# Mask addresses, a reordered tail and one filler matmul less in a decode-attention kernel that streams K and V

## The chip, the cores and the metric

The kernel runs on one core of one Trainium2 chip. The metric is the device time of one execution in microseconds (us). Single runs of one kernel spread over about 1.5 us (before beside e5 to e8: 629.71 to 631.37; e3: 629.97 to 631.48), and this case is about effects of that size, so most of the argument rests on times inside the traces and not on the totals. PE is the matmul engine, DVE the vector engine, ACT the scalar engine; SP issues the loads, and 16 DMA engines carry them out. PE's granted clock is what the trace says that PE ran at: in these traces either full (1.00) or half (0.50); a window that holds a change shows a value between.

## The reference

Grouped-query attention for one new token: 32 query heads share 8 K/V heads, 65,536 keys, head size 128, bf16. The arithmetic is small; K and V are 268.4 MB.

```python
B, Hq, Hkv, Sq, Sk, D = 1, 32, 8, 1, 65536, 128
k = jnp.repeat(k, rep, axis=1); v = jnp.repeat(v, rep, axis=1)
scores = jnp.einsum("bhqd,bhkd->bhqk", q, k) * D ** -0.5
return jnp.einsum("bhqk,bhkd->bhqd", softmax(scores), v)
```

## The kernel before

Each head's keys are cut into two loads (b = 0, 1) of 8.39 MB, laid out as 128 partitions by 256 slots of 128 values. There are two K buffers and one V buffer. All loads are issued by the sync engine (SP) in the order K(g,0), V(g-1,0), K(g,1), V(g-1,1), each as soon as its buffer is free:

```python
def load_k(g, b):
    SP.wait((s_sc, 16 * g - 8 + 8 * b if g else 0))     # scores of the old K are done
...
def load_v(g, b):
    done = 2 * (2 * g + b)
...
        SP.wait((s_vc, done))                            # PE has consumed the old V
        load(v, g, b, 0, s_v[0])
...
for g in range(1, G):
    for b in range(2):
        load_k(g, b)
        load_v(g - 1, b)
```

PE runs a loop over tiles x = 2g+b. A tile is eight parts of scores (eight matmuls each, on K that DVE has transposed in place), then the V matmuls of tile x-2. The addresses of a part come from two counters. The loop body for V has "wide" matmuls (four slots at once, 16 output rows in each of four column groups), and between its first and second half two *filler* matmuls whose result nobody reads:

```python
with block("pe_part"):
    nc.regs_alu(r_n, r_n, 1, op=ALU.add)
    ...
    r_k = (x % 2) * (SL * D) + (n // 2) * (PS * D) + (n % 2) * (2 * D) + SL * D
    r_w = (n % 4) * (-8) + 28
    r_o = (x % 2) * 1024 + (n // 4) * 512
    take(s_kt, 1)                       # wait for the transpose, subtract 1
    ...                                 # eight matmuls at these addresses
with block("pe_values"):
    ...
        if ch == 1:
            i.then_inc(s_vc, 1)
            for _ in range(2):          # the fillers
                pe.matmul(out=pt[0:16, :], lhsT=et[:, 0, 0:16], rhs=et[:, 0, :], start=True, stop=True)
    i.then_inc(s_vb, 1)                 # DVE may fold the wide sums
```

In the last tile V arrives in pieces that end at slots 128, 192, 224, 232, 240, 248, 252, 256. Slots 0 to 231 go through the wide matmuls; their sums are then folded on DVE ("y-sum": a multiply by a 0/1 mask and a reduce over y) and added to the output by the fp32 *gather* matmul. Slots 232 to 255 go one by one through narrow matmuls (4 output rows) straight into the output:

```python
for t in range(SL - TAIL, SL):          # TAIL = 24
    if t == CUTS[5]:
        ...                             # pl: the row sum, fp32
    if t in CUTS:
        pe.wait_ge(s_v[CUTS.index(t)], 16)
    ...                                 # narrow matmul of slot t
pe.wait_ge(s_dv, collected[G - 1])
gather(D, start=False, stop=True).then_inc(s_pe, 1)
```

## Time and profile before

| | before |
|---|---|
| median of 6 runs (lowest to highest) | 630.23 us (629.99 to 630.80) |
| span of the profiled run | 628.0 us |
| load queue, share of 16 engines | 99.1% |
| PE / DVE busy | 56% / 54% |
| last V bytes land | about 624.2 us |
| last matmul ends | 625.33 us |

First some lines of the profile page: the span, PE's busy time (us, share, instructions), the busy share of the DMA engines in 40 slices (tenths), the queue that carries all loads, and the median time from the issue of a full K load to its landing.

```profile
span 628.0 us, 6627 instructions
...
PE 352.5 (56%) x2136; PEld 138.0 (22%) x2136; DVE 339.2 (54%) x131; ACT 36.1 (6%) x32; POOL 7.5 (1%) x40
...
DMA  8999999999999999999999999999999999999996
...
q1 hardware_dynamic: 6656, 268.45, 99.1%
...
io<-in_k_dram SPq DMA_DIRECT2D x13, 43.3
```

The busy digits of DMA are 9 from the second slice to the last but one: the loads bound this kernel, and only what lies before the first and after the last byte, or makes the queue pause, can change the time.

The second view is the timeline of the last 14 us (start, duration, engine, line, operation, output<-input, count, and in brackets the idle time before it and what ended it).

```profile
614.73 3.59 PE L370 MATMUL acc<-io,et 128*16 128x512 bf16 x32 [6.13 <-PEq L113]
...
618.10 1.06 PE L432 MATMUL pt<-et 128*16 128x512 bf16 x2
...
619.63 1.04 PE L370 MATMUL acc<-io,et 128*16 128x512 bf16 x16 [0.47 <-PEq L113]
...
622.03 1.06 PE L370 MATMUL acc<-io,et 128*16 128x512 bf16 x10 [1.36 <-DMA io<-in_v_dram]
...
623.14 0.69 DVE L274 TENSOR_TENSOR vy<-acc,sely 128x512 f32<-128x512 f32 x1 [11.94 <-PE acc L370]
...
623.38 0.61 PE L465 MATMUL pf<-io,et 128*4 128x128 bf16 x8 [0.29 <-DMA io<-in_v_dram]
...
623.86 1.03 DVE L278 TENSOR_REDUCE vs<-vy 128x128 f32<-128x512 f32 x1
...
624.04 1.06 PE L465 MATMUL pf<-io,et 128*4 128x128 bf16 x16
...
624.95 0.38 PE L364 MATMUL pf<-vs,sel 128*4 128x128 f32 x2
625.43 0.36 ACT L331 ACTIVATE o<-pf,rl 4x128 bf16<-4x128 f32 x1 [31.86 <-PE pf L364]
```

Read it by line: L370 are the wide matmuls (32 of slots 0-127 when the first half has landed at 614.73, 16 at 619.63, ten from 622.03), L432 the fillers, L274 and L278 the y-sum, L465 the narrow matmuls, L364 the gather.

The third view is the same timeline around 173 us, in the steady state: the last parts of scores, then the issue of V(1,1), then the moment at which DVE begins on the K load that was the last one in flight.

```profile
165.32 1.92 PE L405 MATMUL acc<-io,wz 128*128 x8 [0.66 <-issue]
...
167.85 1.91 PE L405 MATMUL acc<-io,wz 128*128 x8 [0.61 <-issue]
...
173.80 0.33 SPq L131 DMA_DIRECT2D io<-in_v_dram  x1
...
178.85 4.45 DVE L227 STREAM_TRANSPOSE io<-io 128x4096 uint32<-128x4096 uint32 x1 [21.34 <-DMA io<-in_k_dram]
```

A part takes 2.53 us (165.32 to 167.85), of which 1.92 is matmul and 0.61 a gap on PE.

The fourth view gives busy times of PE and others and the granted PE clock in two stretches just before the tail (columns: PE, weight loads, DVE, ACT, POOL busy us with counts, clock, DMA share, GB/s).

```profile
615.70:619.10 3.40, 3.40 (x30) 0.90 (x18) 0.00 (x0) 0.00 (x0) 0.00 (x0) 0.50 0.96 405
619.10:622.50 3.40, 1.57 (x25) 0.46 (x24) 0.00 (x0) 0.00 (x0) 0.00 (x0) 0.99 1.00 391
```

The clock was half (0.50) in the first stretch, which PE spent busy throughout, and full afterwards.

### The profile page before, as it was taken

How to read it: one execution, taken by the hardware profiler on the slowest of the kernel's cores; microseconds unless marked ns; L12 is line 12 of the kernel's file. 1: busy time of each engine (PE TensorE's matmuls, PEld its weight loads, DVE VectorE, ACT ScalarE, POOL GpSimd, SP SyncE). 2: the span in 40 equal slices, each digit the busy share in tenths (PEclk: the TensorE clock that was granted, in tenths of full speed). 3: DMA queues.
4: the chain of work that ended last, by engine and by line, in shares of the span. 5: the costliest groups of instructions: out<-in, count | busy, mean ns of one | idle time of the engine just before them, and what ended most of it. 6: DMA issues, size and time to landing. Idle time of an engine off the chain costs nothing. (4 is left out here: it accounts for less than half of the span.)

```text
span 628.0 us, 6627 instructions
## 1 busy us (share of the span) xinstructions
PE 352.5 (56%) x2136; PEld 138.0 (22%) x2136; DVE 339.2 (54%) x131; ACT 36.1 (6%) x32; POOL 7.5 (1%) x40
## 2 busy tenths in 40 slices
PE   0676483834838348382573816748176581887335
PEld 0222131311313113130231302213022230332112
DVE  3984835649065490655807558085570846684211
ACT  0000200020000200002000020000200002000100
POOL 1000000000000000000000000000000000000000
PEclk9999596975969759596696966969669595899677
DMA  8999999999999999999999999999999999999996
GB/s 368 434 459 409 459 409 459 409 451 417 451 417 451 417 443 426 442 426 434 434 430 438 422 447 417 451 405 463 401 463 405 463 405 463 399 434 434 434 432 277
DMA packets 6715, 268.48 MB, mean 428 GB/s; under 512 B 825, under 2 KB 1081, under 8 KB 1465
## 3 DMA queue, kind: packets, MB, share of 16 engines
q1 hardware_dynamic: 6656, 268.45, 99.1%
q8 instruction: 1, 0.02, 0.0%
q10 hardware_dynamic: 56, 0.01, 0.0%
q14 instruction: 2, 0.01, 0.0%
HBM read 268.44 MB, written 0.01 MB: 427 GB/s over the span
## 5 line engine op out<-in xcount | busy, mean ns | idle before, releaser
L405 PE MATMUL acc<-io,wz 128*128 x1024 | 270.7, 416 | 179.7 <-issue 92.2
L227 DVE STREAM_TRANSPOSE io<-io 128x4096 uint32<-128x4096 uint32 (+1 forms) x54 | 279.0, 5207 | 161.2 <-DMA io<-in_k_dram 161.2
L405 PEld LDWEIGHTS acc<-io,wz 128*128 x1024 | 105.5, 103 | 345.0 <-issue 267.4
L370 PE MATMUL acc<-io,et 128*16 128x512 bf16 x1018 | 70.6, 409 | 22.3 <-PEq L113 20.9
L232 DVE TENSOR_REDUCE mg<-acc 128x1 f32<-128x2048 f32 x8 | 18.3, 2291 | 55.4 <-PE acc L405 55.4
L246 ACT ACTIVATE ex<-acc,nmb 128x2048 bf16<-128x2048 f32 x8 | 15.7, 1967 | 531.1 <-DVE nmb L244 531.1
L370 PEld LDWEIGHTS acc<-io,et 128*16 128x16 bf16 x1018 | 27.4, 94 | 61.1 <-issue 36.5
L364 PE MATMUL pf<-vs,sel 128*4 128x130 f32 (+1 forms) x20 | 5.7, 386 | 62.4 <-PEq L113 62.4
L268 DVE STREAM_TRANSPOSE et<-ex 128x1024 bf16<-128x1024 bf16 x16 | 19.6, 1225 | 30.0 <-PE acc L370 15.1
L257 ACT ACTIVATE acc<-wz 128x2560 f32<-128x2560 bf16 x7 | 16.1, 2307 | 17.7 <-DVE vs L278 17.6
L364 PEld LDWEIGHTS pf<-vs,sel 128*4 128x4 f32 x20 | 1.1, 83 | 62.8 <-issue 62.8
L236 DVE TENSOR_REDUCE m<-pt 1x4 f32<-1x128 f32 x8 | 2.2, 279 | 21.7 <-PE pt L448 21.7
L350 POOL COPY wz<-qT 32x16 bf16<-32x16 bf16 x32 | 6.1, 190 | 518.2 <-PE acc L405 434.5
L274 DVE TENSOR_TENSOR vy<-acc,sely 128x512 f32<-128x512 f32 x8 | 5.3, 660 | 11.9 <-PE acc L370 11.9
L432 PE MATMUL pt<-et 128*16 128x512 bf16 x32 | 10.0, 395 | 0.0
L278 DVE TENSOR_REDUCE vs<-vy 128x128 f32<-128x512 f32 x8 | 8.2, 1021 | 0.3
L450 PE MATMUL pb<-ident,nrow 1*128 1x1 f32 x8 | 1.6, 194 | 5.7 <-PEq L113 5.7
L432 PEld LDWEIGHTS pt<-et 128*16 128x16 bf16 x32 | 3.0, 94 | 4.4 <-issue 1.1
L448 PE MATMUL pt<-ident,mg 128*1 128x128 f32 x8 | 2.2, 270 | 2.5 <-PEq L113 2.5
L190 DVE MEMSET acc<- 128x2560 f32 x1 | 2.2, 2192 | 1.6 <-SPq L62 1.6
L244 DVE COPY nmb<-pb 128x1 f32<-128x1 f32 x8 | 1.3, 158 | 3.0 <-PE pb L450 3.0
L450 PEld LDWEIGHTS pb<-ident,nrow 1*128 1x128 f32 x8 | 1.1, 138 | 7.0 <-issue 7.0
(26 smaller groups left out, 16.0 us busy)
## 6 DMA issues: line engine op xcount, KB each, us to landing
io<-in_v_dram SPq DMA_DIRECT2D x5, 4096.0 KB, 16.5
io<-in_k_dram SPq DMA_DIRECT2D x4, 4096.0 KB, 25.9
io<-in_k_dram SPq DMA_DIRECT2D x4, 2048.0 KB, 39.8
io<-in_v_dram SPq DMA_DIRECT2D x1, 2048.0 KB, 10.7
io<-in_v_dram SPq DMA_DIRECT2D x1, 1024.0 KB, 12.8
io<-in_v_dram SPq DMA_DIRECT2D x3, 256.0 KB, 13.2
io<-in_v_dram SPq DMA_DIRECT2D x2, 128.0 KB, 13.2
io<-in_k_dram SPq DMA_DIRECT2D x13, 43.3
```

The lines of the kernel that those rows point to most:

```text
L227: dve.transpose(out=part, in_=part).then_inc(s_kt, n // 32)
L232: dve.tensor_reduce(out=mg[:, :], in_=sc, axis=AX.X, op=ALU.max).then_inc(s_mg, 1)
L246: n = ACTQ.mark(act.activation(out=ex[:, :, :].rearrange("p b n -> p (b n)"), in_=sc, func=ACT.Exp, bias=nmb[:, :], scale=SCALE, accum_out ...
L257: cleared[g] = ACTQ.mark(act.activation(out=acc[:, :], in_=wz[:, 0, 0:1].to_broadcast([P, 5 * 512]), func=ACT.Copy))
L268: dve.transpose(out=et[:, :, :].rearrange("p i n -> p (i n)"), in_=ex[:, 2 * b:2 * b + 2, :].rearrange("p i n -> p (i n)"),).then_inc(s_et, 1)
L274: n = DV.mark(dve.tensor_tensor(out=vy[:, :, :], in0=vacc, in1=sely[:, :, None].to_broadcast([P, 4, D]), op=ALU.mult))
L278: return DV.mark(dve.tensor_reduce(out=vs[:, 0:D], in_=vy[:, :, :].rearrange("p y d -> p d y"), axis=AX.X, op=ALU.add))
L350: gp.tensor_copy(out=wz[r, :, c0:c0 + H].rearrange("p (s w) h -> p s w h", s=2), in_=qTb[r, :, :, g, :],).then_inc(s_w, 1)
L364: return pe.matmul(out=pf[0:H, 0:w], lhsT=sel[:, :], rhs=vs[:, 0:w], skip_group_check=True, **kw)
L370: return pe.matmul(out=vacc[32 * c:32 * c + 16, :, :], lhsT=et[:, ch // 2, w0:w0 + 16], rhs=io[:, PS * ch + 4 * tt:PS * ch + 4 * tt + 4, : ...
L405: i = pe.matmul(out=bass.AP(acc, r_o, [[2560, P], [1, 512]]), lhsT=bass.AP(wz, r_w + ((2 * s + e) * WB - 4 * u), [[4 * WB, P], [1, P]]), r ...
L432: pe.matmul(out=pt[0:16, :], lhsT=et[:, 0, 0:16], rhs=et[:, 0, :], start=True, stop=True,)
```

## The change

The intent, as its form shows: cheaper address arithmetic in front of each part; a last y-sum that is ready earlier (contiguous operands, two adds instead of a reduce; a strided layout for the other seven); and less PE work after the last bytes, by moving the row sum ahead of the tail, the gather ahead of the last four slots, and eight more slots into the narrow part. Less conspicuously, one of the two fillers goes, in every tile.

```diff
-TAIL = 24
+TAIL = 32
...
-    vy = sb("vy", [P, 4, D], fp32)
+    vy = sb("vy", [P, D, 4], fp32)
+    vz = vy[:, :, :].rearrange("p d y -> p (d y)").rearrange("p (y d) -> p y d", d=D)
... collect(last): other tiles write vy strided and reduce it contiguously; the last tile:
+        n = DV.mark(dve.tensor_tensor(
+            out=vz[:, 0:2, :], in0=vz[:, 0:2, :], in1=vz[:, 2:4, :], op=ALU.add))
+        DV.after(n)
+        return DV.mark(dve.tensor_tensor(
+            out=vs[:, 0:D], in0=vz[:, 0, :], in1=vz[:, 1, :], op=ALU.add))
... pe_part:
-        r_k = (x % 2) * (SL * D) + (n // 2) * (PS * D) + (n % 2) * (2 * D) + SL * D
-        r_w = (n % 4) * (-8) + 28
-        r_o = (x % 2) * 1024 + (n // 4) * 512
+        nc.regs_alu(r_q, r_q, 8, op=ALU.add)
+        for r, bits in r_q_bits.items():                  # 8, 112, 24, 96
+            nc.regs_alu(r, r_q, bits, op=ALU.bitwise_and)
+        r_k = n8 * (2 * D // 8) + m8 * (PS * D // 16) + SL * D
+        r_w = w8 * (-1) + 28
+        r_o = o8 * 16
... pe_values: one filler instead of two
-                for _ in range(2):
-                    pe.matmul(out=pt[0:16, :], lhsT=et[:, 0, 0:16], ...)
+                pe.matmul(out=pt[0:16, :], lhsT=et[:, 0, 0:16], ...)
... pe_tail: row sum first, gather ahead of the last four slots
+    pe.matmul(out=pl, lhsT=sel[:, :], rhs=vs[...], start=True, stop=True).then_inc(s_pe, 1)
     for t in range(SL - TAIL, SL):
         if t in CUTS:
             pe.wait_ge(s_v[CUTS.index(t)], 16)
+        if t == CUTS[-2]:
+            pe.wait_ge(s_dv, collected[G - 1])
+            gather(D, start=False, stop=False)
```

## The prediction

> **What bounds the kernel now.** DMA does. The page shows the load queue at 99.1% of 16 engines' span, 268.4 MB at 427 GB/s; PE is busy 56%, DVE 54%. By the DMA issues, K loads land a median 43.3 us and V loads 28.6 us after issue, while one 8.39 MB load needs 19.4 us at the 433 GB/s that the windows show: the queue does not run dry. Only about 2 us before the first byte and 4 us after the last can move.

> **The tail before** (timeline, 0.1 us windows; span 628.0). Full DMA rate ends at 623.3, stragglers at 624.2. PE gets slots 224-231 at 622.71 as two wide matmuls, waits for slots 232-239 until 623.38, then never waits: 8 narrow matmuls (66 ns apart), the row-sum matmul (ends 624.02), 16 narrow (to 625.10), the fp32 gather (0.25 us, to 625.34), scaling on ACT 0.36, output store.

> **What the change does.**
> 1. Part addresses by masks: of 2.53 us per part, 1.91 is matmul and 0.62 a gap (timeline). I guess 0.2 to 0.4 us less gap, 128 times, 25 to 50 us of PE time; all off the critical path, as the K reload it triggers is queued over 20 us early. Worth 0.
> 2. The tail's y-sum: the multiply, 0.69 us, stays; the 1.03 us reduce becomes two adds, estimated 0.35 + 0.2 us. It starts at about 622.6, not 623.14, as slots 224-231 leave the wide part. Sum ready about 623.9, not 624.89, where it was nearly limiting (gather weights load at 624.95).
> 3. Eight narrow matmuls more for two wide: +0.3 us PE, but inside the wait that ends at 623.38. Worth 0.
> 4. Row sum first: about 0.1 us of PE leaves the tail. The gather before the last four slots is the same PE work in another order, since PE, not DMA, is last after 623.38.
> Sum: the last matmul ends about 0.1 us earlier, if the clock is full.

> **The risk: one filler matmul fewer.** In the trace the clock changes only on a fixed 3.41 us grid; every cold window that released it was at least 83% PE-busy, and busy shares up to 75% did not. [...] Before, the burst at 614.73 with two fillers runs to 619.16, and the matmuls at 619.63 complete any unlucky window, so the tail is always warm. With one filler it ends near 618.7; for about 4 in 10 phases of the grid no window reaches 80%, and the tail runs at half clock: 28 narrow matmuls after 623.38 at 107 ns instead of 66, plus a slower gather, about +1.3 us. Single runs should fall near 629.9 or near 631.2.

> **Predicted time:** 630.0 us, 629.2 to 631.4 holding it 8 times in 10. Faster by over 2%: 0.003; within 2%: 0.992; slower by over 2%: 0.005.

> **What the profile would show.** DMA share still about 99%. Gap between parts below 0.62 us, PE idle up, span unchanged. The tail's y-sum done before 624.2. Gather before the last four matmuls; last matmul about 1 us after the last byte at full clock, over 2 us at half. In some runs a clock of 0.5 in the last 5 us.

> **What would make it wrong.** PE in time with DMA, so that the last four slots wait for bytes: then moving the gather hides 0.25 us. The threshold lies lower, and no tail is cold. Or the changed pace of PE and DVE changes DMA efficiency itself: 0.1% of rate is 0.6 us, more than the whole tail effect.

The forecast: its sums are 0.1 us earlier at full clock, about 1.3 us later with a tail at half clock. Of its estimates: the 107 ns are a quarter of the 427 ns from one filler to the next at half clock in the trace of before (618.10 us; 512 columns there, 128 in a narrow matmul). The 80% and the "4 in 10 phases" are estimates from the busy shares of the same trace (the highest that stayed at half clock 75.5%, at 458.71 us; the lowest that was followed by full clock 83.2%, at 585.00). What the 0.35 + 0.2 us of the two adds rest on is not said; by the 0.69 us of the multiply on 512 columns, 256 and 128 would be 0.35 and 0.17.

## The result and the profile after

| | before | after |
|---|---|---|
| median of 6 runs | 630.23 us | 630.78 us |
| lowest to highest | 629.99 to 630.80 | 630.05 to 630.95 |
| span of the profiled run | 628.0 us | 628.4 us |
| first half of the last V load used | 614.73 | 615.09 |
| last matmul ends | 625.33 | 625.69 |

The ratio of the two is 1.0005 with a 95% interval of 0.9992 to 1.0018: no difference that these runs can show. (A ratio is the mean time of one kernel's fast runs over that of the other's of the same rounds, so it is not quite the ratio of the medians quoted.) The 0.36 us between the two traces was there before the tail began: the first half of the last V load is used 0.36 us later (615.09 against 614.73), and from there to the last matmul both take 10.60 us.

The page lines that answer to those of before:

```profile
span 628.4 us, 7102 instructions
...
PE 349.1 (56%) x2126; PEld 137.0 (22%) x2126; DVE 339.2 (54%) x132; ACT 36.1 (6%) x32; POOL 7.5 (1%) x40
...
q1 hardware_dynamic: 6656, 268.45, 99.1%
```

There are 475 more instructions although PE and its weight loads lost ten each: the masks are more instructions, not fewer. The listing of one part shows 13 register and control instructions before and 17 after (the wait on the semaphore not counted).

The tail of after:

```profile
615.09 3.59 PE L378 MATMUL acc<-io,et 128*16 128x512 bf16 x32 [6.12 <-PEq L114]
...
618.45 0.63 PE L445 MATMUL pt<-et 128*16 128x512 bf16 x1
...
619.98 1.88 PE L378 MATMUL acc<-io,et 128*16 128x512 bf16 x16 [0.90 <-PEq L114]
...
622.38 1.03 PE L378 MATMUL acc<-io,et 128*16 128x512 bf16 x8 [0.52 <-DMA io<-in_v_dram]
...
623.29 1.92 PE L478 MATMUL pf<-io,et 128*4 128x128 bf16 x28
623.46 0.69 DVE L273 TENSOR_TENSOR vy<-acc,sely 128x512 f32<-128x512 f32 x1 [11.91 <-PE acc L378]
624.19 0.42 DVE L282 TENSOR_TENSOR vy<-vy 128x256 f32<-128x256 f32 x1
624.65 0.29 DVE L286 TENSOR_TENSOR vs<-vy 128x128 f32<-128x128 f32 x1
...
625.09 0.38 PE L372 MATMUL pf<-vs,sel 128*4 128x128 f32 x2
...
625.30 0.39 PE L478 MATMUL pf<-io,et 128*4 128x128 bf16 x4
```

L378 are now the wide matmuls, L445 the filler, L273, L282 and L286 the y-sum, L478 the narrow matmuls, L372 the gather. The eight wide matmuls at 622.38 take 1.03 us; in a trace at full clock they take 0.61 (the run with two fillers, below). So the y-sum starts at 623.46, not the 0.5 us earlier that was planned. The adds take 0.42 and 0.29 us.

The steady state of after, same place as above:

```profile
161.97 1.90 PE L420 MATMUL acc<-io,wz 128*128 x8 [0.68 <-PEq L114]
...
164.50 1.90 PE L420 MATMUL acc<-io,wz 128*128 x8 [0.63 <-PEq L114]
...
172.81 0.33 SPq L132 DMA_DIRECT2D io<-in_v_dram  x1
...
178.47 4.45 DVE L226 STREAM_TRANSPOSE io<-io 128x4096 uint32<-128x4096 uint32 x1 [21.40 <-DMA io<-in_k_dram]
```

The parts still take 2.53 us, the gap is 0.63 here and 0.68 every other time: nothing gained in the gap. But V(1,1) now has 5.66 us in hand instead of 5.05.

And the clock before the tail, in windows that follow the places where the clock changes in this trace:

```profile
616.70:620.10 3.40, 2.50 (x25) 0.73 (x21) 0.00 (x0) 0.00 (x0) 0.00 (x0) 0.50 0.93 393
620.10:623.50 3.40, 2.88 (x29) 0.85 (x22) 0.04 (x1) 0.00 (x0) 0.00 (x0) 0.50 1.01 380
```

With one filler PE was busy 2.50 of 3.40 us (74%) in the first window and the clock stayed at half; the second, 85% busy, released it at 623.5, in the middle of the tail.

Finally the y-sum of the other seven tiles. The group lines (busy us, mean ns) of before and of after:

```profile
L274 DVE TENSOR_TENSOR vy<-acc,sely 128x512 f32<-128x512 f32 x8 | 5.3, 660 | 11.9 <-PE acc L370 11.9
...
L278 DVE TENSOR_REDUCE vs<-vy 128x128 f32<-128x512 f32 x8 | 8.2, 1021 | 0.3
```

```profile
L273 DVE TENSOR_TENSOR vy<-acc,sely 128x512 f32<-128x512 f32 x8 | 7.8, 980 | 11.9 <-PE acc L378 11.9
...
L279 DVE TENSOR_REDUCE vs<-vy 128x128 f32<-128x512 f32 x7 | 4.8, 686 | 0.2
```

The strided write makes the multiply dearer (median 652 to 1016 ns; the mean of after includes the last tile) and the contiguous reduce cheaper (1021 to 686 ns): the sum stays at 1.7 us.

### The profile page after: what moved, and what is told of

Read it like the earlier page. It is cut to its first block, busy times and chain, and to the rows that moved or that the text cites. A ratio compares the mean times of both kernels' runs of the same rounds, so it can differ in the third digit from the quotient of the medians.

```text
span 628.4 us, 7102 instructions
## 1 busy us (share of the span) xinstructions
PE 349.1 (56%) x2126; PEld 137.0 (22%) x2126; DVE 339.2 (54%) x132; ACT 36.1 (6%) x32; POOL 7.5 (1%) x40
## 3 DMA queue, kind: packets, MB, share of 16 engines
q1 hardware_dynamic: 6656, 268.45, 99.1%
## 5 line engine op out<-in xcount | busy, mean ns | idle before, releaser
L378 PE MATMUL acc<-io,et 128*16 128x512 bf16 x1016 | 69.0, 416 | 22.1 <-PEq L114 21.5
L372 PE MATMUL pf<-vs,sel 128*4 128x130 f32 (+1 forms) x20 | 5.7, 386 | 62.6 <-PEq L114 62.6
L378 PEld LDWEIGHTS acc<-io,et 128*16 128x16 bf16 x1016 | 26.3, 94 | 61.4 <-issue 38.2
L372 PEld LDWEIGHTS pf<-vs,sel 128*4 128x4 f32 x20 | 1.2, 83 | 63.0 <-issue 63.0
L273 DVE TENSOR_TENSOR vy<-acc,sely 128x512 f32<-128x512 f32 x8 | 7.8, 980 | 11.9 <-PE acc L378 11.9
L445 PE MATMUL pt<-et 128*16 128x512 bf16 x16 | 6.6, 410 | 0.0
L279 DVE TENSOR_REDUCE vs<-vy 128x128 f32<-128x512 f32 x7 | 4.8, 686 | 0.2
L292 ACT ACTIVATE fall<-pf 4x130 f32<-4x130 f32 x7 | 1.9, 269 | 7.7 <-PE pf L372 7.7
```

Of the source, the lines that this page charges most:

```text
L273: n = DV.mark(dve.tensor_tensor(out=vy[:, :, :].rearrange("p d y -> p y d") if not last else vz, in0=vacc, in1=sely[:, :, None].to_broadca ...
L279: return DV.mark(dve.tensor_reduce(out=vs[:, 0:D], in_=vy[:, :, :], axis=AX.X, op=ALU.add))
L372: return pe.matmul(out=pf[0:H, 0:w], lhsT=sel[:, :], rhs=vs[:, 0:w], skip_group_check=True, **kw)
L378: return pe.matmul(out=vacc[32 * c:32 * c + 16, :, :], lhsT=et[:, ch // 2, w0:w0 + 16], rhs=io[:, PS * ch + 4 * tt:PS * ch + 4 * tt + 4, : ...
```

## The experiments

Twelve kernels ran, in three sets of four, each set on one chip with its own runs of the kernel before in the same rounds (9, 11 and 9 runs; means 630.32, 630.43 and 630.45 us). All results were correct. This table puts them side by side. "Landing" is when PE starts on the first half of the last V load, "tail" the time from there to the end of the last matmul, "in hand" the time from the issue of a V load (the one between 401 and 413 us) to DVE's start on the K load then in flight; all from the traces. "Clock" is the granted clock while the narrow matmuls run.

| kernel | mean us of n runs (lowest to highest) | landing | tail | clock | in hand |
|---|---|---|---|---|---|
| before | 630.33, 6 (629.99 to 630.80) | 614.73 | 10.60 | full | 5.11 |
| after | 630.65, 6 (630.05 to 630.95) | 615.09 | 10.60 | half to 623.5 | 5.65 |
| e1 after again | 630.85, 5 (630.08 to 631.47) | 614.93 | 11.60 | half 622.6 to 626.0 | 5.66 |
| e2 two fillers | 630.30, 5 (630.11 to 630.61) | 614.86 | 10.57 | full | 5.49 |
| e3 masks only | 630.30, 5 (629.97 to 631.48) | 614.54 | 10.62 | full | 5.43 |
| e4 constant addresses | 630.55, 5 (630.26 to 630.97) | 615.01 | 10.60 | full | 9.97 |
| e5 no filler | 630.59, 5 (630.08 to 631.69) | 614.47 | 10.85 | half to 623.7 | 5.95 |
| e6 six fillers | 631.83, 6 (630.28 to 633.45) | 615.97 | 10.57 | full | 4.62 |
| e7 tail only | 630.82, 5 (630.15 to 631.70) | 615.09 | 11.56 | half 622.6 to 626.0 | 5.09 |
| e8 before, one filler | 630.58, 5 (630.11 to 631.24) | 615.18 | 11.25 | half 622.3 to 625.7 | 5.36 |
| e9 fillers in last tile | 630.15, 5 (630.03 to 630.41) | 614.42 | 10.58 | full | 5.87 |
| e10 gather in the wait | 630.37, 5 (630.03 to 630.49) | 615.19 | 10.41 | full | 5.93 |
| e11 six fillers, constants | 630.59, 5 (630.09 to 630.90) | 615.34 | 10.55 | full | 9.11 |
| e12 twelve fillers | 637.04, 5 (635.27 to 638.04) | 622.63 | 10.53 | full | 3.55 |

The tail column is the cleanest result. At full clock it is 10.60 to 10.62 us for the old tail (before, e3, e4) and 10.53 to 10.58 for the new one (e2, e6, e9, e11, e12): 0.05 us apart in the mean. It is longer only where the clock was half.

### e1: the changed kernel once more

No edit.

> The changed kernel itself, unchanged, for its spread and a second trace. Theory (the loads bound the kernel and the change touches only the last 3 us): ratio to before 0.9990 to 1.0010, single runs spread over about 1 us, and the difference between the two kernels' spans equals the difference of the times at which their last V bytes land, to 0.15 us. Rival (the change made it really slower by 0.05% or more): ratio at or above 1.0005 with an interval that leaves out 1.

Measured: ratio 1.0005 (0.9992 to 1.0019); runs of 630.08, 630.44, 631.02, 631.25 and 631.47. Its trace fell into another phase of the clock, and shows what half a clock costs:

```profile
619.10:622.50 3.40, 1.30 (x24) 0.46 (x24) 0.00 (x0) 0.00 (x0) 0.00 (x0) 0.99 1.00 394
622.50:625.90 3.40, 3.40 (x39) 3.20 (x32) 1.48 (x4) 0.00 (x0) 0.00 (x0) 0.51 0.35 114
```

```profile
622.92 3.15 PE L478 MATMUL pf<-io,et 128*4 128x128 bf16 x28
...
625.86 0.45 PE L372 MATMUL pf<-vs,sel 128*4 128x128 f32 x2
...
626.14 0.39 PE L478 MATMUL pf<-io,et 128*4 128x128 bf16 x4
```

The clock had been released at 619.1. In the window to 622.5 PE was busy only 1.30 of 3.40 us, and the clock was taken away again for 622.6 to 626.0, which is nearly the whole tail. The 28 narrow matmuls take 3.15 us instead of 2.16 in e2, where that includes waits for V. What follows: my first theory (the spans differ by the landing of the loads alone) is wrong for this run. Landing differs from before by 0.20 us, the span by 1.2; the missing 1.0 is the tail (11.60 against 10.60).

### e2: two fillers on the changed kernel

```diff
-                pe.matmul(out=pt[0:16, :], ...)
+                for _ in range(2):
+                    pe.matmul(out=pt[0:16, :], ...)
```

> The changed kernel with the second filler matmul back. Theory: the clock is full from 621 us on in the trace whatever the phase of the grid; the wide matmuls of slots 192-223 take about 0.65 us instead of 1.03, the y-sum starts 0.35 us earlier after its bytes, and the last matmul ends 1.0 to 1.2 us after the last byte. Total 0 to 0.3 us shorter than the changed kernel, within the noise. Rival (the filler matters not at all): same clock pattern as with one filler.

Measured: ratio 0.9999 (0.9985 to 1.0012), highest run 630.61. Full clock from 619.9, the eight wide matmuls 0.61 us, last byte (624.32 by the packet records of the trace) to last matmul 1.11 us, 1.10 in before. As expected for this phase. The tail, 10.57 us, is 0.03 us shorter than before's 10.60: that is all that the new order of the tail is worth here at full clock.

### e3: masks only, on the kernel before

```diff
-        r_k = (x % 2) * (SL * D) + (n // 2) * (PS * D) + (n % 2) * (2 * D) + SL * D
+        for r, bits in r_q_bits.items():
+            nc.regs_alu(r, r_q, bits, op=ALU.bitwise_and)
+        ...                                   # as in the change; all else as before
```

> The kernel before with only the addresses by masks. Theory after seeing the trace: the gap between two parts stays 0.60 to 0.70 us (before 0.62, after 0.66), as four AND instructions and a compare mask replace the compound address instructions one for one or worse; total ratio 0.999 to 1.001. Rival (masks are cheaper and the gap of after is widened by something else): gap 0.2 to 0.5 us.

Measured: ratio 1.0000 (0.9987 to 1.0014); gaps of 0.64 to 0.68 us between parts. The gap is not shorter. What the masks do bring is in the last column: 5.43 us in hand instead of 5.11. The masks stand ahead of the wait for the transpose, so the first part of a tile starts sooner after DVE (in the tile at 140 us, where a pair of transposes takes 17.30 us and the first is taken as half of that: 1.18 us after its end in before, 150.03 against 148.85, and 0.73 in after, 149.14 against 148.41). It is a gain in latency, of about 0.3 us per tile, and nobody waits for it. After has 5.65 us in hand; the other 0.2 us fits the filler that is missing there (0.216 us from one filler to the next at full clock, before at 171.42).

### e4: constant addresses, on the kernel before

```diff
+    def parts(b):
+        for n in range(8):                     # written out, b = 0 and b = 1
+            r_k = b * (SL * D) + (n // 2) * (PS * D) + (n % 2) * (2 * D) + SL * D
+            ...
+    with block("pe_pick"):
+        nc.regs_alu(r_n, r_x, 2, op=ALU.mod)
+        nc.br_cmp(r_n, 0, "pe_part0", "pe_part1", "IS_EQ", engines=only)
```

> The kernel before with the sixteen parts written out with constant addresses, no address arithmetic at all; the result stays right. If address arithmetic makes the gap between parts, the gap falls from 0.62 to 0.3 us or less; if the wait-and-subtract on the semaphore and the refill of the queue make it, it stays above 0.5 us. Either way the total ratio is 0.999 to 1.001, since PE is not what the loads wait for; the rival (PE pace changes the rate of the loads) expects 0.3% or more.

Measured: ratio 1.0004 (0.9990 to 1.0017). The gap is gone:

```profile
149.35 15.88 PE L399 MATMUL acc<-io,wz 128*128 128x512 bf16 x64 [11.55 <-PEq L113]
...
169.27 0.33 SPq L131 DMA_DIRECT2D io<-in_v_dram  x1
...
179.17 4.45 DVE L227 STREAM_TRANSPOSE io<-io 128x4096 uint32<-128x4096 uint32 x1 [21.38 <-DMA io<-in_k_dram]
```

64 matmuls in 15.88 us without a break, so address arithmetic and the loop made the gap of 0.62 us, and the wait on the semaphore did not. V(1,1) is issued with 9.90 us in hand. The kernel is not faster for it. This settles the first part of the change: even removing all of the arithmetic buys nothing, because the loads don't wait for PE when 5 us are in hand.

### e5: no filler on the changed kernel

```diff
-                pe.matmul(out=pt[0:16, :], ...)
```

> The changed kernel with no filler matmul at all. Theory (the filler decides in how many runs the tail has half clock): from the busy times of the traces, a release share of 76 to 82% and a throttle share of 40 to 46% of a 3.41 us window, an estimate gives 4 to 7 of 10 phases of the grid with a late tail, by up to 1.6 us, and a mean 0.4 to 0.8 us above the kernel with six fillers. Rival (the spread of a run is all from the loads, the filler does nothing): mean within 0.2 us of the kernel with six fillers.

Measured: mean 630.59, ratio 1.0003 (0.9990 to 1.0017), one run of 631.69, and a trace at half clock until 623.7 with a tail of 10.85. The comparison it was meant for failed, since the kernel with six fillers turned out slow for another reason. Against e2 (630.30) the totals don't decide: the landing differs by 0.9 us between traces (614.42 to 615.34), and half a clock cost 0.3 us in this one. e9, six fillers in the last tile alone, has a mean 0.44 us lower, but ran on another chip.

### e6: six fillers on the changed kernel

```diff
+                for _ in range(6):
+                    pe.matmul(out=pt[0:16, :], ...)
```

> The changed kernel with six fillers, which run from 618.2 past the landing of slots 128 to 191 at 619.8. Theory: full clock in the tail in every phase, last matmul 0.9 to 1.2 us after the last byte in the trace, mean equal to the kernel before to 0.2 us; six fillers at half clock end near 620.9 at the latest, before slots 192 to 223 land at 622.2, so they cost nothing. Rival: as for the kernel without filler, the same mean.

Measured: ratio 1.0022 (1.0007 to 1.0038), slower by an interval that leaves out 1, though far within 2%; five of six runs above 631.4, where none of 11 runs of before in these rounds was. My expectation that fillers cost nothing fell. The tail is as it should be (10.57 us, full clock); the loads landed late (615.97). The extra fillers run in all tiles, and V(g,1) is issued with 4.6 us in hand, 0.5 less than in before and 1.0 less than in after. That gave two new theories: B, V is issued too late to keep the queue full; C, PE's activity itself disturbs the loads. e11 and e12 tell them apart.

### e7: the new tail alone

The kernel before with the new tail and y-sum, the old addresses and two fillers.

```diff
 # the change, less these:
-        ...bitwise_and addresses
-                pe.matmul(...)                # one filler
+        r_k = (x % 2) * (SL * D) + ...
+                for _ in range(2):
+                    pe.matmul(...)
```

> The kernel before with the new tail (32 single slots, y-sum in three passes, row sum first, gather ahead of the last four), the old addresses and two fillers. Theory: tail at full clock, 0.9 to 1.1 us from last byte to last matmul as before (1.13 in the trace of before), total ratio 0.9990 to 1.0005: the new order of the tail is worth 0 to 0.15 us, because after slots 240 to 247 land PE still has 16 narrow matmuls and the gather to do in any order. Rival (the new order hides the gather, 0.25 us or more): last byte to last matmul 0.8 us or less.

Measured: ratio 1.0002 (0.9989 to 1.0015). The expectation was missed: tail 11.56 us, at half clock, with two fillers. In the window 619.1 to 622.5 PE was busy 1.47 us of 3.40 (43%), and the clock went; in the trace of before, in the same phase, 1.57 us (46%) kept it. So two fillers don't always suffice: slots 192 to 223 were used later here (622.38, against 622.03 there), and less of their work fell into the window. My claim that the old kernel's tail "is always warm" was made for its own tail, and all traces of that tail with two fillers are warm (before, e3, e4); but a share of 46% is no safe one: elsewhere in these traces a window of 42% kept the clock (e1, from 404.12 us) and one of 45% lost it (after, from 128.61).

### e8: one filler on the kernel before

```diff
-                for _ in range(2):
-                    pe.matmul(out=pt[0:16, :], ...)
+                pe.matmul(out=pt[0:16, :], ...)
```

> The kernel before with one filler instead of two, nothing else. Theory: the same loss as in the changed kernel, an estimate of 1 to 3.5 of 10 phases with a late tail by up to 1.1 us, mean 0.1 to 0.3 us above before; so hard to see in the total, but some runs near 631 and a trace that may show a half clock after 621 us. Rival: no difference in the distribution.

Measured: ratio 0.9999 (0.9986 to 1.0012), so nothing in the total, as foretold; the trace has half clock from 622.3 to 625.7 and a tail of 11.25 us, so the loss is not tied to the new tail.

### e9: six fillers in the last tile alone, on the changed kernel

```diff
+        nc.br_cmp(r_x, 2 * G + 1, "pe_upper", "pe_fill", "IS_LT", engines=only)
+    with block("pe_fill"):
+        for _ in range(6):
+            pe.matmul(out=pt[0:16, :], ...)
+        nc.br("pe_upper", engines=only)
```

> The changed kernel with six fillers in the last tile alone and none in the other fifteen. Theory A (the slowdown of six fillers everywhere, 1.4 us in the mean, came from the main loop, where the loads fell 1.1 to 1.8 us behind, and the tail gains by a full clock): full clock from 619 us on in the trace, last byte to last matmul 0.9 to 1.1 us, mean 629.9 to 630.5 and at or below the mean of before, none of the runs above 631.4 but by the jitter of the loads. Rival (fillers in the last tile themselves delay the end): mean above 631.

Measured: ratio 0.9996 (0.9983 to 1.0010), runs from 630.03 to 630.41, the narrowest spread and the lowest mean of all twelve. Full clock from 618.1, tail 10.58 us, 5.87 us in hand. As theory A expected. It is not faster than before by an interval that leaves out 1; what the trace shows is that both risks, the cold tail and the late V, are absent in it.

### e10: the gather inside a wait

On top of e9:

```diff
-TAIL = 32
-CUTS = [0, 128, 192, 224, 232, 240, 248, 252, 256]
+TAIL = 40
+CUTS = [0, 128, 192, 216, 224, 232, 240, 248, 252, 256]
...
-        if t in CUTS:
-            pe.wait_ge(s_v[CUTS.index(t)], 16)
-        if t == CUTS[-2]:
+        if t == CUTS[-4]:
             pe.wait_ge(s_dv, collected[G - 1])
             gather(D, start=False, stop=False)
+        if t in CUTS:
+            pe.wait_ge(s_v[CUTS.index(t)], 16)
```

> As the kernel with fillers in the last tile, and the wide matmuls end at slot 216, so that the y-sum is ready before slots 240 to 247 land, and the gather stands ahead of the wait for them, where the trace with two fillers shows PE idle for 0.2 us. Theory: the gather leaves the path, last byte to last matmul 0.7 to 0.9 us instead of 1.03, total 0.1 to 0.3 us shorter, which the total will hardly show. Rival (PE has no room there, or one more load costs as much): no shorter.

Measured: ratio 0.9999 (0.9986 to 1.0013). The tail:

```profile
624.31 0.38 PE L372 MATMUL pf<-vs,sel 128*4 128x128 f32 x2
...
624.55 1.05 PE L483 MATMUL pf<-io,et 128*4 128x128 bf16 x16
```

The gather runs at 624.31, before the 16 narrow matmuls of the last slots, and the tail is 10.41 us, 0.17 shorter than e9's 10.58. It is the shortest of all twelve. From last byte to last matmul it is 0.91 us by the packet records, against 1.10 in e9, at the edge of what was expected. 0.17 us is 0.03% of the time, and the totals can't show it.

### e11: six fillers everywhere, with constant addresses

The edits of e4 and e6 together, on the changed kernel.

> Six fillers in every tile, but part addresses as constants, which by the trace let V(g,1) be issued 4 us earlier (169.3 instead of 173.8 us), so with about twice the time in hand before the queue could run dry. Theory B (the fillers slow the loads by issuing V later, 0.7 us of the 4 us in hand): the mean falls back to 630.3 to 630.9. Theory C (the activity of PE itself disturbs the loads): the mean stays at 631.4 or more.

Measured: mean 630.59, ratio 1.0002 (0.9988 to 1.0016). V has 9.11 us in hand and the slowdown of six fillers is gone. This is theory B: PE does the same matmuls as in e6, and they alone do no harm. (e6 and e11 ran on different chips, each against its own runs of before.)

### e12: twelve fillers, six in the last tile

```diff
+        for _ in range(6):                     # all tiles
+            pe.matmul(out=pt[0:16, :], ...)
+        # six more in all tiles but the last
```

> The changed kernel with six fillers in the last tile and twelve in each of the others: the suspected cost doubled. Theory B or C: V(g,1) is issued 1.3 us later still, and the mean rises further, to 632 or more, with the loss in the landing of the loads and not in the tail. Rival (the slowdown with six fillers was the jitter of one set of rounds): mean within 0.5 us of before.

Measured: ratio 1.0101 (1.0084 to 1.0118), 637.04 us in the mean. The tail is 10.53 us; the loads land at 622.63, 7.9 us after before's.

```profile
177.12 0.33 SPq L132 DMA_DIRECT2D io<-in_v_dram  x1
...
180.40 4.45 DVE L226 STREAM_TRANSPOSE io<-io 128x4096 uint32<-128x4096 uint32 x1 [21.39 <-DMA io<-in_k_dram]
```

V(1,1) has 3.28 us in hand. DVE begins on the K load that follows it in the queue at 221.03, 40.63 us after 180.40, against 39.11 in before (178.85 to 217.96): 1.5 us lost in this pair of loads, 2.4 in a later one (259.33 to 300.40, against 256.26 to 294.96). The other V(g,1) of e12 have 2.9 to 3.7 us in hand. From 66 to 566 us the loads run at 433 GB/s in before, 431 in e6 and 426 in e12.

That the queue pauses can be read from the packet records of the kept traces (start and duration of every DMA packet). In before all 16 DMA engines have a packet in flight, but for gaps under 0.1 us, while V(1,1) is issued and K lands (172 to 182 us), and around the later V(g,1) too. In e6 up to two of them have none from 176.70 to 177.57 and from 254.46 to 256.12, although V had been issued 2 us before; in e12 up to 11 have none between 177.37 and 178.28, and up to 15 between 335.39 and 337.64. So the engines do not finish a load together: some run dry before the last one lands, and the time in hand, which counts to the last, says too much.

In the mean, then, before lost nothing that shows with 4.7 to 5.1 us in hand, e6 with 4.4 to 4.6 lost 1.4 us, and e12 with 2.9 to 3.7 lost 6.6. That is an order, not a threshold: in e6's trace only the two loads with the least in hand (4.56 and 4.43) are followed by a longer pair of loads, and the three with 4.6 are not.

## Why the prediction was right or wrong

The time (630.0 foretold, 630.78 measured, range 629.2 to 631.4) and "within 2%" held. This says little: 2% is 12.6 us in a kernel of which I saw 6 us that could move, and the range is wider than the spread of single runs. That steps 2 and 3 below did no harm was luck: the arithmetic was costed wrongly, and the slack behind it was smaller than I thought. By steps:

1. **The loads bound the kernel.** Right: 99.1% of the span before and after. From 66 to 566 us the traces of before and of after both show 433 GB/s, with the 16 DMA engines busy all the time (share 1.00).
2. **"I guess 0.2 to 0.4 us less gap, 128 times".** Wrong. The gap is 0.63 to 0.68 us after, 0.61 to 0.66 before. The masks are 17 register and control instructions per part instead of 13, and e4 shows that these, with the loop, are the gap. I costed an operation by its name and did not count instructions.
3. **"All off the critical path, as the K reload it triggers is queued over 20 us early".** The conclusion held and the reason was wrong. I took the medians of issue to landing (43.3 and 28.6 us) for the time in hand. K is issued right behind V, and V is what must come in time: in before the V loads of odd tiles have 4.7 to 5.1 us. e4 shows that more is worth nothing, e6 and e12 that less costs: 1.4 us in the mean for 0.5 us. Had the masks made a tile 0.5 us longer instead of 0.3 shorter, it would by this estimate have stood about where e6 stands.
4. **The y-sum.** Its adds took 0.42 + 0.29 us, not 0.35 + 0.2. At full clock it was ready earlier: in e2 at 624.29, 9.43 us after the landing, against 624.89 and 10.16 us in before. As the whole tail shortened by only 0.03 us, the y-sum had not been what ended it. I did not foresee that the other seven y-sums would trade 0.36 us of multiply for 0.34 us of reduce.
5. **"The last matmul ends about 0.1 us earlier, if the clock is full".** Mis-sized by half: 0.05 us (five traces of the new tail at full clock, 10.53 to 10.58, against three of the old, 10.60 to 10.62). After slots 240 to 247 have landed, 16 narrow matmuls and the gather are left in both kernels. Only e10 takes the gather out of that stretch.
6. **The filler.** What was foretold was seen: changes of the clock on a 3.41 us grid, half clock in the tail of after, e1, e5 and e8. Counted over the fourteen traces, the tail has half clock in all four with no filler or one, in one of five with two (e7), and in none of five with six in the last tile. The cost was foretold as 1.3 us; against full clock on the same tail it was 1.0 (e1 and e7), 0.65 (e8), 0.3 (e5) and 0.04 (after), by how much of the tail the half clock covers. The narrow matmuls were 107 ns apart at half clock (e1), as foretold; at full clock they follow each other at 56 ns (before, from 623.38), not 66, but PE then waits for pieces of V (e2: 28 of them in 2.16 us), so less than the difference is lost. I had only considered that the clock is not released. In e1, e7 and e8 it was released and taken away again, for a window that was 37 to 43% busy, which I had not looked for; and on the new tail not even two fillers always suffice (e7).
7. **"Single runs should fall near 629.9 or near 631.2".** Not so. Both kernels have runs all over 630.0 to 631.5, as the landing of the last load alone ran from 614.42 to 615.34 in the traces other than e6 and e12. The 11 runs of the changed kernel (the result and e1) have a mean of 630.74, the 35 of before in all four sets 630.39; this fits a loss of a few tenths from the clock, but these runs are from different chips and rounds and do not show it.

What stays open: why the loads' landing varies by up to 1 us between runs even with 9 us in hand (e4, e11). The traces narrow it: DVE begins on K(3,1) at 255.96 us in e9 and at 256.90 in e11, and from there to the landing all but e6, e12 and e10 take 358.44 to 358.48 us (e10 lost 0.87 us in one pair of loads with 6.1 us in hand); so the difference arises in the first 256 us. Open too are the shares of runs with a cold tail (half clock), of which each kernel left one or two traces only. The state of the clock in the runs without a trace is not known.

## What to carry to other kernels

When a queue of loads is full, measure how many microseconds each load is issued before the queue would be empty, load by load and not by the median: this kernel had 5 us where I had read over 20 from the medians, and 0.5 us less cost 1.4 us in the mean (e6), more than the 0.17 us by which the shortest tail (e10) beat e9's. Count instructions before calling an arithmetic rewrite cheaper, and ask who waits for them. And work that looks useless may be holding a clock (here the tail had half clock in all four traces with no filler or one, and in none of the five with six in the last tile): when removing it, look at several traces for the clock at the end, and give the tail its own warm-up (e9) where the loop has no time to spare.
